# Gated mix of sliding-window attention and a GELU MLP: maxima begin sooner, V is kept by feature, and half of the repeated high parts are written by copies in DRAM

## The chip, the cores and the metric

The kernel runs on one core of one Trainium2 chip. The metric is the device time of one launch in microseconds; below it is 750.38 us, the median of three runs (749.24 to 751.35). The profile is of one further execution.

## What is computed

For x of 2048 rows and 512 features (all inputs in float32):

```python
g = sigmoid((x * gate_w).sum(-1, keepdims=True))
q, k, v = split_heads(x @ wqkv)              # 32 heads of 16 features
s = (q @ k.T) / 4, masked to 0 <= row - col < 256
a = merge(softmax(s) @ v) @ wo
b = gelu(x @ w1 + b1) @ w2 + b2              # 1792 hidden features
out = g * a + (1 - g) * b
```

## The kernel before, in words

The matrix products are made almost as exact as float32 from three products of rounded numbers: each operand is cut into a high part and a rest (both fp32r), and `mm3` (L107 to L110) issues high x high, high x rest, rest x high. Three such matmuls of 512 columns are called a step here (`MM3`); the dense work is a stream of steps.

**The order of the work is written out by one program.** `gated_mix` runs a model of time, `now`, in ns. `tick(ns)` lets it pass, `after(ns, fn)` puts an operation into a list by its due time, `need(key)` runs that list until something is done. Each engine executes its instructions in the order in which they were put out. `dense()` is a generator of all dense work: qkv for four quarters of 512 rows (`t` = 0 to 3), eight turns of the MLP (`TURNS`: half of the hidden features for one quarter; seven blocks of u, then four blocks of y), and the output projection (`final`, called a). `fill(ns)` takes that many ns of steps from it.

**Attention** runs over 8 groups of 4 heads (`g_`) and 16 blocks of 128 rows, 128 units `u` in all. After `fill(START)` a loop over the units begins. Each pass puts out four maxima (`att_max`, tile sm: a matmul of q and k, then DVE takes the row maximum with the mask added, L524), four scores (`att_exp`, tile st: a matmul that subtracts the maximum in its product, then ACT's exponential into tile pt, L586, and the cut of the window by POOL at L580, or by DVE at L574 for the last 12 units), and dense steps between them (2750 ns a pass before the first score, 2330 ns after). The maxima are `LEAD` = 12 units ahead of the scores. After every fourth unit `att_pvs` multiplies pt with V, 8 small tiles of 64 x 32 side by side in the array (L608, in plain float32, 96 records or, for the first rows of a group, 72). Column 16 of V is 1, so the same product gives the softmax's denominator. The sums (nd) go to DRAM, are divided there and back (`att_norm`) and come back as ot for the projection. When the loop ends, the rest of `dense()` follows.

**What lies where.** qkv writes q and k to DRAM (SQ, SK) as three parts, because attention's products take 48 rows: rest, high, high for q; high, rest, high for k. `qk_out` stores the first two parts with one DMA (L329) and the repeated high part with a second one from the same SBUF tile (L330). `qkv_v` evicts V of one block of 128 rows with four ACT instructions into a tile vx of 17 columns a head, the last set to 1 by POOL (L338), and stores it with three DMAs (L357, L359). `att_load_v` (L505) loads, for a group and a quarter, 128 x 8 x 34 numbers into one half of `vbuf`; a weight load of L608 takes 32 neighbouring columns. `load_qd`, `load_kd`, `load_ks`, `load_qs` load q and k of a group. All DMAs are issued by SP, in one queue, in program order. While the last quarter's qkv and the first MLP turn run, the MLP's weights are loaded and cut (`split`, L178 on ACT, L182 on DVE or POOL). PSUM holds three sm, three st and two dense tiles (d).

Of the kernel before, what the change touches and what calls it, by code (L numbers as in the profile page):

```python
# [9 lines left out]
F32 = mybir.dt.float32  # L10
F32R = mybir.dt.float32r
BF16 = mybir.dt.bfloat16
AF = mybir.ActivationFunctionType
# [4 lines left out]
S, D, F, H, DH, W = 2048, 512, 1792, 32, 16, 256  # L18
T = 512
NT = S // T  # L20
NB = T // 128
# [3 lines left out]
NG = H // 4  # L25
# [7 lines left out]
def gated_mix(ctx: ExitStack, tc: tile.TileContext, x, wqkv, wo, w1, b1, w2, b2, gate_w, out):  # L33
    nc = tc.nc
# [11 lines left out]
    def f32(ap):  # L46
        return ap.bitcast(F32)

    tt = cp.tile([128, 2 * RB, 32], F32, name="tt")
    mask = cp.tile([128, 320], BF16, name="mask")  # L50
    qs = cp.tile([128, 2, S], F32R, name="qs")
# [3 lines left out]

    idle = cs.tile([128, 320], BF16, tag="jm", bufs=1, name="idle")
    nc.gpsimd.memset(idle, 0.0)
# [3 lines left out]
    SK = [dr.tile([H // NC, 16, 3, NC, T], F32, name=f"SK{t}") for t in range(NT)]  # L61
    SV = [dr.tile([128, NB, 2, H // 2 * 17], F32, name=f"SV{t}") for t in range(NT)]
    XT = [dr.tile([NC, 128, 2, T], F32, name=f"XT{t}") for t in range(NT)]
# [17 lines left out]

    cut = cs.tile([128, 2, 64], F32, name="cut")
    nc.gpsimd.memset(cut, 3e38)
    for r in (0, 64):
# [15 lines left out]
    nc.gpsimd.memset(f32(nms), 0.0)  # L100
# [138 lines left out]

    xts, xrs = {}, {}  # L240

# [72 lines left out]
    def qk_out(t, j, p):  # L314

        dst, i = (SQ[t], j) if j < NC else (SK[t], j - NC)
        e = sb.tile([128, 2, T], F32R, tag="h", bufs=7, name=f"qke{t}_{j}")

        h = 1 if j < NC else 0

        def hi():
            nc.scalar.activation(e[:, h], p, AF.Copy)  # L322

        def lo():
            nc.vector.tensor_sub(e[:, 1 - h], p, f32(e[:, h]))  # L325

        def store():
            to = dst[:, :, :, i].rearrange("h d s c -> (h d) s c")
            nc.sync.dma_start(to[:, 0:2], f32(e))  # L329
            nc.sync.dma_start(to[:, 2], f32(e[:, h]))  # L330
            done.add(("qk", t, j))
        after(100, hi), after(700, lo), after(700 + HOLDQ, store)

    def qkv_v(t, b):
        xt = xts[t]
        vx = f32(sb.tile([128, 2, T], F32R, tag="h", bufs=7, name=f"vx{t}_{b}"))
        vx = vx.rearrange("p s t -> p (s t)")[:, 0:H * 17].rearrange("p (h c) -> p h c", c=17)
        nc.gpsimd.memset(vx[:, :, 16:17], 1.0)  # L338

        p = ps.tile([128, D], F32, tag="d", bufs=2, name=f"v{t}_{b}")  # L340
        ts = slice(b * 128, (b + 1) * 128)
        for c in range(NC):
            w = wt["v", c]
            mm3(p, xt[:, c, 0, ts], xt[:, c, 1, ts], w[:, 0], w[:, 1], c == 0, c == NC - 1)
            yield MM3
        def ev():
            to = vx[:, :, 0:16].rearrange("p (s i g a) d -> p i s g a d", i=2, s=2, a=2)
            by = p.rearrange("p (i a g s d) -> p i s g a d", i=2, a=2, s=2, d=16)
            for i in range(2):
                for s in range(2):  # L350
                    nc.scalar.activation(to[:, i, s], by[:, i, s], AF.Copy)
            after(HOLDQ, store)

        def store():
            flat = vx.rearrange("p h c -> p (h c)")
            n = H // 2 * 17
            nc.sync.dma_start(SV[t][:, b, 1], flat[:, n:2 * n])  # L357
            for r in (0, 64):
                nc.sync.dma_start(SV[t][64 - r:128 - r, b, 0], flat[r:r + 64, 0:n])  # L359
            done.add(("v", t, b))  # L360
        after(100, ev)
# [139 lines left out]
    def att_load_v(g_, c):  # L501
        need(*[("v", c, b) for b in range(NB)])
        vt = vbuf[:, c % 2]
        dst = vt[:, 0:NB * 68].rearrange("p (j c) -> p j c", c=34)
        nc.sync.dma_start(dst, SV[c].rearrange("p j s c -> p (j s) c")[:, :, 34 * g_:34 * g_ + 34])  # L505
        vts[g_, c] = vt

    def att_max(g_, b, i):

        if b % RB == 0 and (g_, b // RB) not in Ms:  # L510
# [9 lines left out]
                         start=True, stop=True)  # L520
        junk = cs.tile([128, 320], BF16, tag="jm", bufs=1, name=f"jm{g_}_{b}_{i}")

# [69 lines left out]
    def att_pvs(u):  # L592
# [12 lines left out]
        def mm(b, i, hf, q, e, rhs, start, stop):  # L605
            r = 64 * (1 ^ hf ^ i % 2)
            v = 68 * (b % NB) + 17 * (i % 2 * 2 + i // 2)
            nc.tensor.matmul(pv[r // 64][32 * i:32 * i + 32, q - c * T:e - c * T],  # L608
                             vts[g_, b // NB][r:r + 64, v:v + 32], rhs(r),
                             start=start, stop=stop, skip_group_check=True, tile_position=(r, 32 * i))  # L610
# [400 lines left out]
```

## Time and profile before

| | |
|---|---|
| median of three runs | 750.38 us (749.24 to 751.35) |
| the profiled execution | 752.58 us |
| its span, first to last instruction | 750.6 us |
| PE / DVE / ACT / POOL busy | 98% / 69% / 57% / 50% |
| granted TensorE clock | full throughout |
| DMA: packets, bytes | 179258, 172.10 MB; 56672 packets under 512 bytes |
| share of the DMA queue of SP | 81% of 16 engines' span |
| first maximum on PE | 119.9 us |
| first / last PV section on PE | 182.5 us / 699.5 us |

A row of a profile names the engine, the line, the operation and out<-in by the program's tile names. PEld is the loading of weights into the array, which overlaps PE; SPq is SP's issuing of a DMA. Matmul ends are modelled, so where PE stands still is read from how long equal stretches of work take, and from the list of waits, more than from the busy share.

### The profile page before, as it was taken

Reading aid. Unit: us, or ns where it says so; the run is one execution under the profiler, and the core shown is the slowest. Engines: PE = TensorE matmul, PEld = TensorE weight load, DVE = VectorE, ACT = ScalarE, POOL = GpSimd, SP = SyncE. Lnnn points to the kernel's source line nnn. Section 1 sums busy time; section 2 is a strip of 40 time slices with the busy share of each in tenths; the row PEclk is TensorE's granted clock in tenths of the full one; section 3 lists DMA queues with packets and bytes.
Section 4 is the critical chain, followed back from the end, with each engine's and each line's share of the span. In section 5 each row is a group of like instructions: output and inputs, shape, how many; then the busy total and the mean of one; then the engine's idle time right before and its main releaser. Section 6 shows DMA issues by size and latency. Waiting matters only on the chain.

```text
span 750.6 us, 17969 instructions
## 1 busy us (share of the span) xinstructions
PE 733.8 (98%) x6129; PEld 605.3 (81%) x6129; DVE 519.6 (69%) x1567; ACT 430.9 (57%) x972; POOL 372.0 (50%) x846
## 2 busy tenths in 40 slices
PE   8999999998999999999999999999999999999998
PEld 6888888876788888888887877888888888878787
DVE  4532325789758867986898689868867886784552
ACT  4434522358547845864696478547845854785541
POOL 4200000339756765786577657757865875630000
PEclk9999999999999999999999999999999999999999
DMA  9889798998995687799576889996799898538783
GB/s 315 328 275 402 258 387 274 254 316 186 272 253 141 153 242 203 186 226 263 143 180 167 214 230 219 253 243 153 179 259 246 203 237 217 135 88 263 226 265 115
DMA packets 179258, 172.10 MB, mean 229 GB/s; under 512 B 56672, under 2 KB 122976, under 8 KB 179168
## 3 DMA queue, kind: packets, MB, share of 16 engines
q1 hardware_dynamic: 179168, 170.97, 81.0%
q8 instruction: 48, 0.79, 0.5%
q14 instruction: 42, 0.34, 0.2%
HBM read 108.53 MB, written 62.39 MB: 228 GB/s over the span
## 4 chain that ended last, share of the span: by engine, by line
PE 83%; DMA 6%; DVE 4%; ACT 2%; issue 2%; SPq 1%; POOL 0%; DVEq 0%; ACTq 0%; POOLq 0%
PE sm L519 9%; PE st L564 8%; PE y L108 7%; PE pv_sm L608 6%; PE y L110 6%; PE y L109 6%; PE u L108 5%; PE u L109 5%; PE u L110 5%; PE qk L110 4%; PE qk L108 4%; PE qk L109 4%; PE v L108 2%; PE a L108 2%; PE v L110 2%
## 5 line engine op out<-in xcount | busy, mean ns | idle before, releaser
L524 DVE CUSTOM_DVE_ANT_0 jm<-sm,mask 128x320 bf16<-128x320 f32 (+4 forms) x512 | 237.9, 465 | 83.4 <-PE sm L519 55.7
L580 POOL TENSOR_SCALAR_AFFINE_SELECT pt<-pt 64x256 f32<-64x256 f32 (+1 forms) x538 | 225.8, 440 | 118.6 <-ACT pt L586 108.2
L586 ACT ACTIVATE pt<-st 128x320 f32<-128x320 f32 (+4 forms) x512 | 207.1, 425 | 131.7 <-PE st L564 128.4
L519 PE MATMUL sm<-kd,qd 96*128 96x320 f32 (+4 forms) x512 | 156.3, 308 | 6.1 <-DVE M L524 3.8
L564 PE MATMUL st<-qs,ks 128*128 128x320 f32 (+4 forms) x512 | 155.7, 307 | 1.2 <-ACT pt L586 1.2
L546 POOL CAST qs<-tt 4x256 fp32r<-4x256 f32 x256 | 126.2, 493 | 42.4 <-DVE tt L539 31.4
L519 PEld LDWEIGHTS sm<-kd,qd 96*128 96x128 f32 x512 | 96.1, 188 | 34.3 <-DVE M L524 10.9
L564 PEld LDWEIGHTS st<-qs,ks 128*128 128x128 f32 x512 | 97.2, 190 | 21.5 <-ACT pt L586 2.3
L108 PE MATMUL y<-w,h 128*128 128x512 f32 x224 | 89.9, 401 | 0.0
L110 PE MATMUL y<-w,h 128*128 128x512 f32 x224 | 88.4, 395 | 0.3 <-DVE h L737 0.3
L109 PE MATMUL y<-w,h 128*128 128x512 f32 x224 | 88.2, 394 | 0.0
L108 PE MATMUL u<-mx,w 128*128 128x512 f32 x196 | 80.0, 408 | 0.0
L109 PE MATMUL u<-mx,w 128*128 128x512 f32 x196 | 77.3, 394 | 0.0
L110 PE MATMUL u<-mx,w 128*128 128x512 f32 x196 | 77.2, 394 | 0.0
L608 PE MATMUL pv_st<-pt,vbuf 64*32 64x320 f32 (+4 forms) x1408 | 73.2, 346 | 2.5 <-DVE pt L574 1.3
L608 PE MATMUL pv_sm<-pt,vbuf 64*32 64x320 f32 (+4 forms) x1408 | 74.1, 346 | 0.1
L608 PEld LDWEIGHTS pv_sm<-pt,vbuf 64*32 64x32 f32 x1408 | 51.1, 106 | 19.1 <-issue 2.3
L325 DVE TENSOR_TENSOR qke<-qk,qke 128x512 fp32r<-128x512 f32 x32 | 22.1, 690 | 47.4 <-ACT qke L322 39.3
L322 ACT ACTIVATE qke<-qk 128x512 fp32r<-128x512 f32 x32 | 19.1, 598 | 55.6 <-PE qk L110 32.3
L110 PEld LDWEIGHTS y<-w,h 128*128 128x128 f32 x224 | 42.1, 188 | 10.7 <-DVE h L737 1.2
L608 PEld LDWEIGHTS pv_st<-pt,vbuf 64*32 64x32 f32 x1408 | 46.0, 106 | 2.8 <-DVE pt L574 1.5
L338 POOL MEMSET vx<- 128x32 f32 x16 | 2.4, 156 | 89.2 <-DMA SQ<-qke 42.9
(148 smaller groups left out, 1334.4 us busy)
## 6 DMA issues: line engine op xcount, KB each, us to landing
kd<-SK SPq DMA_DIRECT2D x32, 384.0 KB
qs<-SQ SPq DMA_DIRECT2D x64, 192.0 KB
mx<-XT SPq DMA_DIRECT2D x24, 512.0 KB
SQ<-qke SPq DMA_DIRECT2D x16, 512.0 KB
SK<-qke SPq DMA_DIRECT2D x16, 512.0 KB
ND<-nd SPq DMA_DIRECT2D x32, 256.0 KB
raw_w<-in_B_w_dram SPq DMA_DIRECT2D x28, 256.0 KB
ks<-SK SPq DMA_DIRECT2D x32, 192.0 KB
```

The lines of the kernel that those rows point to most:

```text
L108: nc.tensor.matmul(p, lh, rh, start=first, stop=False)
L109: nc.tensor.matmul(p, lh, rl, start=False, stop=False)
L110: nc.tensor.matmul(p, ll, rh, start=False, stop=last)
L322: nc.scalar.activation(e[:, h], p, AF.Copy)
L325: nc.vector.tensor_sub(e[:, 1 - h], p, f32(e[:, h]))
L519: nc.tensor.matmul(p[:, :w], qd[0:96, n, pr, 128 * j:128 * (j + 1)], kd[0:96, n, pr, k1 - w:k1], start=True, stop=True)
L524: nc.vector.tensor_tensor_reduce(junk[:, :w], p[:, :w], mask[:, 320 - w:320], 1.0, -3e38, ALU.add, ALU.max, M[:, 2 * (b % RB) + hb, pr:pr ...
L546: nc.gpsimd.tensor_copy(dst, src.unsqueeze(1).broadcast_to([4, 2, RB, 32]))
L564: nc.tensor.matmul(p[:, :w], ks[:, slot(g_, kb // NB), pr, at:at + 128], qs[:, pr, k0:k0 + w], start=True, stop=True)
L580: nc.gpsimd.affine_select(out=v, in_=v, pattern=[[0, v.shape[1]], [1 - 2 * e, 64]], compare_op=ALU.is_ge, fill=0.0, base=-e, channel_multi ...
L586: nc.scalar.activation(pt[:, hf, pr, :w], p[:, :w], AF.Exp, scale=SCALE)
L608: nc.tensor.matmul(pv[r // 64][32 * i:32 * i + 32, q - c * T:e - c * T], vts[g_, b // NB][r:r + 64, v:v + 32], rhs(r), start=start, stop=s ...
```

## The change

Three things change together.

1. `START` goes from 105000 to 97000 ns: the attention loop begins 8 us of dense work sooner. Nothing else in the loop changes.
2. V lies in DRAM by feature: per quarter, `SV` is [2, 128, 8, 128]; for a head parity, a row and a group it holds 16 features x 4 blocks x 2 heads. The four blocks of a quarter are evicted into two tiles that stay until the last block is done, with a step of 8 numbers between features, and are stored with three DMAs a quarter of 4 KB rows. A load for a group and a quarter has 256 pieces of 512 bytes. The ones are set once at the start, behind each of the four V regions of `vbuf`. A weight load takes every eighth number, 32 of them: 16 features, a one, and whatever lies behind (results of those 15 columns are not used). So that this stays finite, `cut` (now filled with 1e30) and `mask` lie in the same tile as V.
3. For the groups 4 to 7 (`i >= 2`), the repeated high part is not stored from SBUF. A DMA copies it from the first part in DRAM, with due times 188000, 196000, ... 308000 ns.

```diff
-    SV = [dr.tile([128, NB, 2, H // 2 * 17], F32, name=f"SV{t}") for t in range(NT)]
+    SV = [dr.tile([2, 128, NG, NB * 32], F32, name=f"SV{t}") for t in range(NT)]
...
+    vbuf = cs.tile([128, 4 * VB + 288], F32, name="vbuf")
+    cut = vbuf[:, 2 * VB:2 * VB + 128].rearrange("p (e x) -> p e x", e=2)
+    mask = vbuf[:, 4 * VB + 128:].bitcast(BF16)
...
-    vbuf = cs.tile([128, 2, NB * 68 + 16], F32, name="vbuf")
-    nc.gpsimd.memset(vbuf[:, :, NB * 68:], 0.0)
+    nc.gpsimd.memset(vbuf[:, 0:2 * VB], 1.0)
+    nc.gpsimd.memset(vbuf[:, 2 * VB + 128:4 * VB + 128], 1.0)
...
             nc.sync.dma_start(to[:, 0:2], f32(e))
-            nc.sync.dma_start(to[:, 2], f32(e[:, h]))
-            done.add(("qk", t, j))
+            if i < 2:
+                nc.sync.dma_start(to[:, 2], f32(e[:, h]))
+                done.add(("qk", t, j))
+            else:
+                copies[0] += 1
+                after(COPY0 + COPY * copies[0] - now[0], copy, to)
+
+        def copy(to):
+            nc.sync.dma_start(to[:, 2], to[:, h])
+            done.add(("qk", t, j))
...
-        nc.gpsimd.memset(vx[:, :, 16:17], 1.0)
...
-            for i in range(2):
-                for s in range(2):
-                    nc.scalar.activation(to[:, i, s], by[:, i, s], AF.Copy)
-            after(HOLDQ, store)
+            for s in range(2):
+                to = vxs[t, s].rearrange("p (i g d b a) -> p i g b a d", i=2, b=NB, a=2, d=16)
+                for i in range(2):
+                    nc.scalar.activation(to[:, i, :, b], by[:, i, s], AF.Copy)
+            if b == NB - 1:
+                after(HOLDQ, store)
...
+        k = (2 * VB + 128) * (c % 2)
+        vt = vbuf[:, k:k + 2 * VB].rearrange("p (s x) -> p s x", s=2)[:, :, 0:NB * 32]
+        nc.sync.dma_start(vt, SV[c][:, :, g_].rearrange("s p x -> p s x"))
...
-            v = 68 * (b % NB) + 17 * (i % 2 * 2 + i // 2)
+            v = vts[g_, b // NB] + VB * (i % 2) + 2 * (b % NB) + i // 2
...
-                             vts[g_, b // NB][r:r + 64, v:v + 32], rhs(r),
+                             vbuf[r:r + 64, v:v + 32 * 8 - 7:8], rhs(r),
...
+COPY0 = 180000.0
+COPY = 8000.0
+VB = NB * 32 + 8
...
-START = 105000.0
+START = 97000.0
```

What the smaller START moves on PE, at the first score (st_0_0, unit 0). Before, it stands in the third block of u of the first MLP turn, after the maxima of units 0 to 11:

```order
L110 MATMUL u_2_1740<-xt_1009,w_2_1421 128x512
L519 MATMUL sm_12_1_1770<-kd,qd 128x320
L564 MATMUL st_0_0_1774<-qs,ks 128x320
L108 MATMUL u_2_1740<-xt_1009,w_2_1421 128x512
L109 MATMUL u_2_1740<-xt_1009,w_2_1421 128x512
L110 MATMUL u_2_1740<-xt_1009,w_2_1421 128x512
L519 MATMUL sm_12_0_1789<-kd,qd 128x320
L564 MATMUL st_0_1_1794<-qs,ks 128x320
```

Of the change, the same place is in the last qkv block, just ahead of the first block of u:

```order
L111 MATMUL qk_7_1597<-xt_970,qk_427 128x512
L532 MATMUL sm_12_1_1622<-kd,qd 128x320
L577 MATMUL st_0_0_1628<-qs,ks 128x320
L109 MATMUL qk_7_1597<-xt_970,qk_427 128x512
L110 MATMUL qk_7_1597<-xt_970,qk_427 128x512
L111 MATMUL qk_7_1597<-xt_970,qk_427 128x512
L532 MATMUL sm_12_0_1643<-kd,qd 128x320
L577 MATMUL st_0_1_1646<-qs,ks 128x320
L109 MATMUL u_0_1652<-xt_970,w_0_1290 128x512
```

The dense work has moved back by about two blocks and a half against the attention. In the first stretch of u there are now 33 maxima, 33 scores and two PV sections, where there were 31, 21 and one.

On SP, at the loads of q for the first two maxima chunks (qd of group 0, quarters 0 and 1). Before, they stand behind loads of ks and two blocks of V of the third quarter:

```order
L475 DMA ks<-SK_84 48x7x128
L477 DMA ks<-SK_84 48x2x64
L357 DMA SV_89<-vx_1_1111 128x272
L359 DMA SV_89<-vx_1_1111 64x272 x2
L480 DMA qd<-SQ_79 48x8x128
L475 DMA qd<-SQ_79 48x7x128
L477 DMA qd<-SQ_79 48x2x64
L480 DMA qd<-SQ_80 48x8x128
L475 DMA qd<-SQ_80 48x7x128
L477 DMA qd<-SQ_80 48x2x64
```

Of the change:

```order
L331 DMA SQ_81<-qke_3_1013 128x2x512
L493 DMA qd<-SQ_79 48x8x128
L488 DMA qd<-SQ_79 48x7x128
L490 DMA qd<-SQ_79 48x2x64
L493 DMA qd<-SQ_80 48x8x128
L488 DMA qd<-SQ_80 48x7x128
L490 DMA qd<-SQ_80 48x2x64
L331 DMA SK_85<-qke_7_1037 128x2x512
L493 DMA ks<-SK_83 48x8x128
L488 DMA ks<-SK_83 48x7x128
L490 DMA ks<-SK_83 48x2x64
```

They now stand right behind the store of the third quarter's last q block; ks and V's stores come later.

At the end of the attention on PE, the last scores (st_15) and the first of the last PV section. Before, the MLP's last y matmul stands ahead of the last score:

```order
L109 MATMUL y_13_10414<-w_13_6717,h_13_10098 128x512
L110 MATMUL y_13_10414<-w_13_6717,h_13_10098 128x512
L564 MATMUL st_15_3_10474<-qs,ks 128x64
L608 MATMUL pv_3_sm<-pt_10_10237,vbuf 32x64
L608 MATMUL pv_3_st<-pt_15_10452,vbuf 32x64
```

Of the change, one step of y stands between them, and eleven more follow the section:

```order
L111 MATMUL y_12_10352<-w_8_6305,h_8_9857 128x512
L577 MATMUL st_15_3_10369<-qs,ks 128x64
L109 MATMUL y_12_10352<-w_9_6404,h_9_9908 128x512
L110 MATMUL y_12_10352<-w_9_6404,h_9_9908 128x512
L111 MATMUL y_12_10352<-w_9_6404,h_9_9908 128x512
L621 MATMUL pv_3_sm<-pt_10_10108,vbuf 32x64
L621 MATMUL pv_3_st<-pt_15_10342,vbuf 32x64
```

More of the change, by code (lines that the diff above doesn't have):

```diff
@@ L49, in gated_mix @@
     tt = cp.tile([128, 2 * RB, 32], F32, name="tt")
-    mask = cp.tile([128, 320], BF16, name="mask")
+    idle = cp.tile([128, 320], BF16, tag="jm", bufs=1, name="idle")
     qs = cp.tile([128, 2, S], F32R, name="qs")
@@ L80, in gated_mix @@
                                 compare_op=ALU.is_ge, fill=NEG, base=0, channel_multiplier=1)
-    cut = cs.tile([128, 2, 64], F32, name="cut")
-    nc.gpsimd.memset(cut, 3e38)
+    nc.gpsimd.memset(cut, 1e30)
     for r in (0, 64):
@@ L238, in clear_q @@
         nc.scalar.activation(v, nil.broadcast_to([128, 2 * T]), AF.Copy)
-    xts, xrs = {}, {}
+    copies = [0]
+    xts, xrs, vxs = {}, {}, {}
     def load_xr(t, bs=range(NB)):
@@ L335, in qkv_v @@
         xt = xts[t]
-        vx = f32(sb.tile([128, 2, T], F32R, tag="h", bufs=7, name=f"vx{t}_{b}"))
-        vx = vx.rearrange("p s t -> p (s t)")[:, 0:H * 17].rearrange("p (h c) -> p h c", c=17)
-        nc.gpsimd.memset(vx[:, :, 16:17], 1.0)
+        if b == 0:
+            for s in range(2):
+                v = f32(sb.tile([128, 2, T], F32R, tag="h", bufs=7, name=f"vx{t}_{s}"))
+                vxs[t, s] = v.rearrange("p s t -> p (s t)")
         p = ps.tile([128, D], F32, tag="d", bufs=2, name=f"v{t}_{b}")
@@ L502, in att_load_v @@
         need(*[("v", c, b) for b in range(NB)])
[L503 to L506, printed above, removed]
+        k = (2 * VB + 128) * (c % 2)
+        vt = vbuf[:, k:k + 2 * VB].rearrange("p (s x) -> p s x", s=2)[:, :, 0:NB * 32]
+        nc.sync.dma_start(vt, SV[c][:, :, g_].rearrange("s p x -> p s x"))
+        vts[g_, c] = k
     def att_max(g_, b, i):
@@ L520, in att_max @@
                          start=True, stop=True)
-        junk = cs.tile([128, 320], BF16, tag="jm", bufs=1, name=f"jm{g_}_{b}_{i}")
+        junk = cp.tile([128, 320], BF16, tag="jm", bufs=1, name=f"jm{g_}_{b}_{i}")
         def red():
```

17 lines of the change are left out of this document (9 added, 8 removed).

## The prediction

> **What bounds the kernel now.** I read the page first.
>
> ```profile
> span 750.6 us, 17969 instructions
> PE 733.8 (98%) x6129; PEld 605.3 (81%) x6129; DVE 519.6 (69%) x1567; ACT 430.9 (57%) x972; POOL 372.0 (50%) x846
> L524 DVE CUSTOM_DVE_ANT_0 jm<-sm,mask 128x320 bf16<-128x320 f32 (+4 forms) x512 | 237.9, 465 | 83.4 <-PE sm L519 55.7
> ```
>
> PE is busy for 98% of the span, and the maxima are DVE's costliest group. The matmul ends are modelled, so 98% does not say how many microseconds can still be won. For that I cut the dense work into its stretches: a turn of the MLP is seven blocks of u (its first product, 12 matmuls a block), then four blocks of y (21 each), eight turns over. A stretch of u and one of y both hold 84 dense matmuls of 512 columns; only the attention between them differs. A step is three dense matmuls. In the windows view the columns are length, busy time with instruction count of PE, PEld, DVE, ACT and POOL, granted clock, DMA share, GB/s. In order: u and y of the first turn, the shortest later u, a later y, u with y of turn 4, u of turn 5, u and y of the last turn, the output projection.
>
> ```profile
> 151.90:186.40 34.50, 31.49 (x210) 24.39 (x209) 30.85 (x93) 25.23 (x52) 20.89 (x37) 1.00 0.96 241
> 186.40:222.60 36.20, 34.78 (x344) 28.50 (x343) 24.17 (x85) 17.73 (x41) 24.65 (x62) 1.00 0.97 269
> 290.40:323.80 33.40, 33.40 (x320) 28.14 (x319) 29.93 (x93) 25.65 (x58) 23.01 (x48) 1.00 0.76 185
> 256.40:290.40 34.00, 34.00 (x343) 28.41 (x341) 23.42 (x83) 17.29 (x39) 22.49 (x60) 1.00 0.86 238
> 358.50:393.20 34.70, 34.03 (x321) 28.25 (x320) 30.46 (x93) 27.47 (x62) 23.94 (x50) 1.00 0.68 161
> 393.20:428.20 35.00, 34.43 (x341) 28.17 (x341) 26.90 (x90) 18.79 (x43) 24.56 (x61) 1.00 0.75 187
> 428.20:465.50 37.30, 35.51 (x321) 28.01 (x320) 32.96 (x98) 28.63 (x65) 23.66 (x50) 1.00 0.91 221
> 636.00:668.40 32.40, 32.27 (x305) 26.06 (x304) 26.44 (x72) 25.96 (x60) 19.45 (x39) 1.00 0.42 112
> 668.40:703.40 35.00, 31.98 (x405) 25.50 (x403) 19.37 (x41) 20.29 (x48) 0.00 (x0) 1.00 0.70 218
> 703.40:747.10 43.70, 43.70 (x212) 36.62 (x204) 21.20 (x33) 16.83 (x28) 0.00 (x0) 1.00 0.61 206
> ```
>
> The first u stretch holds 210 PE instructions against 320, yet takes 34.5 us against 33.4. The missing ones are score matmuls (st) and PV matmuls; these are their rows, st in the first u and in the one at 290.4, then L608 in both.
>
> ```profile
> 151.90:186.40 34.50, 6.82 (x21) 3.98 (x21) 8.38 (x20) 1.00 0.96 241
> 290.40:323.80 33.40, 9.97 (x34) 6.28 (x33) 12.86 (x33) 1.00 0.76 185
> 151.90:186.40 34.50, 1.98 (x72) 1.49 (x72) 1.00 0.96 241
> 290.40:323.80 33.40, 4.37 (x168) 3.04 (x168) 1.00 0.76 185
> ```
>
> What they cost PE, from its timeline: one 320-column sm or st each 0.15 us (333.39 to 333.54), and a PV section of 96 records 2.32 us (333.79 until y starts at 336.11).
>
> ```profile
> 333.39 0.31 PE L519 MATMUL sm<-kd,qd 96*128 96x320 f32 x1
> 333.54 0.31 PE L564 MATMUL st<-qs,ks 128*128 128x320 f32 x1
> 333.79 0.25 PE L608 MATMUL pv_st<-pt,vbuf 64*32 64x64 f32 x2
> 333.87 0.22 PE L608 MATMUL pv_st<-pt,vbuf 64*32 64x64 f32 x2
> 333.93 0.33 PE L608 MATMUL pv_st<-pt,vbuf 64*32 64x192 f32 x2
> 334.52 0.44 PE L608 MATMUL pv_st<-pt,vbuf 64*32 64x320 f32 x2
> 334.79 0.44 PE L608 MATMUL pv_st<-pt,vbuf 64*32 64x320 f32 x2
> 336.11 0.50 PE L108 MATMUL y<-w,h 128*128 128x512 f32 x1
> ```
>
> So without stalls the first u stretch would be 33.4 - 14 x 0.15 - 2.32 = 29.0 us: **5.5 us stand still there**. The first y is 36.2 against 34.0 + 0.3 for one sm and one st more: 1.9 us. The last u would be 33.4 - 16 x 0.15 = 31.0 (1.4 lost), and the last y, without 32 sm and with a third section, 34.0 - 4.8 + 2.3 = 31.5 (3.5 lost). The projection at the end has no gap (43.70 busy of 43.70). The waits of PE name who is late:
>
> ```profile
> PE sm L519 <- DVE M L524: 3.8, 10, 0.8
> PE pv_st L608 <- DVE pt L574: 1.3, 1, 1.3
> ```
>
> DVE holds sm buffers until their maxima are taken. In the first u stretch it is busy 30.85 of 34.5 us with 93 instructions, which leaves 0.04 us between two of them: no room. It has the maxima, the gelu of seven blocks and weight splits (L182) together, while PE's own work there is short. That, not a transfer, is the first thing late.
>
> **The change, part by part.**
>
> *Maxima sooner.* START falls by 8 us of dense work: the order puts every maximum and score 12 steps earlier, so the first u stretch now holds 33 maxima, 33 scores and two PV sections, exactly what the stretches at 290.4 and 358.5 hold. PE's work there is then 33.4 us instead of 29.0, and DVE gets 4.4 us more time for two more maxima and one more nd sum. The splits stay: four on DVE before and after. L182 in the first u, at 358.5 and at 428.2 (DVE, then POOL):
>
> ```profile
> 151.90:186.40 34.50, 3.76 (x5) 2.58 (x2) 1.00 0.96 241
> 358.50:393.20 34.70, 3.17 (x4) 0.00 (x0) 1.00 0.68 161
> 428.20:465.50 37.30, 4.32 (x6) 0.00 (x0) 1.00 0.91 221
> ```
>
> The row at 358.5 has the same attention and four splits on DVE: 34.7 us, 1.3 of stall. The row at 428.2 has six, and a DMA share of 0.91: 37.3 us, 3.9. The first u has four on DVE and two on POOL at a share of 0.96, so it is no nearer to the one than to the other: I take the middle, 2.6 us, which is **-2.9 us** (ends -4.2 and -1.6; -5.5 if no stall is left). The y behind it inherits less lag; the y behind the split-laden u at 358.5 took 35.0, 1.0 over its 34.0, so 1.9 becomes 1.0: **-0.9** (0 to -1.9). The maxima taken sooner lie in qkv of the last quarter, whose first four blocks get 16 maxima instead of 7.
>
> ```profile
> 113.10:124.90 11.80, 11.80 (x57) 9.82 (x56) 5.57 (x24) 2.67 (x8) 0.32 (x2) 1.00 0.79 228
> ```
>
> Nine more at 0.465 us and a read of 0.08 bring DVE to 10.5 us and, with 42 gaps of 0.04, 12.2; PE then works 11.8 + 9 x 0.15 = 13.2. It fits: 0 (to +1).
>
> At the end the attention finishes 11 steps before the MLP does. One step of y (0.7 us) now stands between the last score and the last PV section, which waited 1.3 us for its cut: -0.7. The projection's first load (L703), due two blocks into the last y, falls behind most exponentials instead of among them: about -0.5, an estimate, since ACT waits in order for it. Against it, the last u loses 14 more maxima (PE 28.8 us by the same sum) while ACT keeps its 25.96 us busy and 60 instructions, some 28.4 with gaps: ACT is then the bound, +0.7. Net **-0.5** (-2 to +2). The 8 us moved behind the attention are PE-bound and were PE-bound before; the projection's tail only gets more slack.
>
> *First maxima's loads.* SP issued qd of the first group at 114.11 and PE used it at 119.88.
>
> ```profile
> 102.09 1.10 SPq L329 DMA_DIRECT2D SQ<-qke  x1
> ...
> 114.11 0.53 SPq L480 DMA_DIRECT2D qd<-SQ  x1
> 119.88 0.20 PE L519 MATMUL sm<-kd,qd 96*128 96x64 f32 x1
> ```
>
> PE now wants it 12 steps of 0.68 us (43.70 us by 64 steps of projection), 8.2 us, sooner: at 111.7. In the new order qd stands right behind the store of qke_3, the row at 102.09, and ks and the V stores stand behind it. Six loads at 0.53 us are issued by about 106, still 5.7 us ahead: 0 us (up to +4 if they land late, since a maximum that waits holds all of PE behind it).
>
> *V by feature.* Twelve V stores a quarter become three; each of the 32 loads becomes 256 pieces of 512 bytes instead of 1024 of 136. No PE wait names vbuf or SV, so 0; SP's queue and the DMA engines gain room before 190 us, where their share is 0.96. If it does move PE, it moves it towards the bigger gain below. Sixteen memsets on POOL go, off the chain. The evictions now write with a step of 32 bytes: four of 0.28 us a block against 2.7 us of matmuls (four steps) and two buffers, hidden even at twice that (bounds 0 to +0.5).
>
> ```profile
> L351 ACT ACTIVATE vx<-v x64: 272/281/297, 35.1 to 139.1; 128x128 f32<-128x128 f32 x64
> ```
>
> Two memsets of 128x272 replace a small one in POOL's setup, ahead of the first weight copy, which PE waits for:
>
> ```profile
> 5.45 0.31 POOL L100 MEMSET nm<- 128x256 f32 x1
> 5.88 0.61 POOL L194 CAST qk<-raw_qk 128x512 fp32r<-128x512 f32 x1
> 6.55 0.74 PE L310 MATMUL qk<-ks,qk 128*128 128x256 f32 x4 [0.98 <-POOL qk L194]
> ```
>
> Two at the pace of the nm memset (next start 0.25 us later) for one at 0.18: **+0.35** (0.1 to 0.5), nothing hides it.
>
> *Weights with a step.* L608 now loads 32 columns that lie 32 bytes apart; before, they were neighbours. No load with a step is in the trace. The rows nearest:
>
> ```profile
> L608 PEld LDWEIGHTS pv_sm<-pt,vbuf 64*32 64x32 f32 x1408 | 51.1, 106 | 19.1 <-issue 2.3 <-DVE M L524 0.9 <-DVE nm L536 0.8
> L110 PEld LDWEIGHTS y<-w,h 128*128 128x128 f32 x224 | 42.1, 188 | 10.7 <-DVE h L737 1.2
> ```
>
> 96 columns more cost 82 ns, so 32 columns are 27 ns of the 106. Wide passes follow each other after 270 ns (334.52 to 334.79) and hide any of this; narrow ones after 80 and 60 (333.79, 333.87, 333.93), so with the first load three are open per section. At twice the time a column that is 3 x 27 ns x 32 sections = 2.6 us, at four times 7.8. I take 0, since loads run beside the matmuls and bring a column in 0.85 ns, slower already than the 0.47 ns at which a 320-column matmul reads its columns (0.15 us); ends 0 and +7.8. [...]
>
> *Copies in DRAM.* Sixteen stores of 128x512 leave the four quarters of qkv; sixteen copies are issued on SP between about 190 and 320 us, among transfers with shares of 0.76 to 0.97. Each reads what was stored 100 us or more before, so SP does not wait for it; behind it stand scores' and V's loads. 0, at worst +1.0, the stall by which 35.0 exceeds 34.0.
>
> **Sum.** -2.9 - 0.9 - 0.5 + 0.35 = -3.95 us. The profiled execution took 752.58 us (span 750.6), 2.2 above the median of the three runs; 752.58 becomes 748.6, the median 750.38 becomes **746.4**.
>
> **Rivals.** (1) *The weight step costs.* Slower: at four times a column, 746.4 + 7.8 = 754.2. It decides from a load of about 171 ns: 65 ns more x 3 x 32 = 6.2 us, which eats the gain and 0.3% more. For it: each column is read from another place; against: loads overlap wide passes. At twice, 749.0. (2) *DVE stays the bound*, because gelu, maxima and splits meet anyway, as at 428.2, and the y and the end give nothing: -1.6 + 0.35, 749.1; for it the DMA share of 0.96, against it the row at 358.5. (3) *Relief is worth more*: the stalls of the first u and y and 2 us at the end all go, since transfers are fewer: -5.5 - 1.9 - 2 + 0.35 = 741.3. (4) *START buys nothing*: qd lands late, PE waits up to 4 us in front of the first maximum, and DVE's crowd only moves: 749.1 + 4 = 753.1.
>
> **Chances.** Forecast (743.5 to 748.5) 0.50, (1) four times 0.10 and twice 0.08, (2) 0.16, (3) 0.08, (4) 0.08. A measurement here tells about 0.3%, 2.25 us, from no change. Faster by more: 0.46 + 0.08 of (3) = 0.54. Slower by more: 0.10 + 0.06 of (4) + 0.04 of (2) with the copies or the end at their worst = 0.20. Within: 0.26. Range 741.3 to 754.2: from (3) to (1).
>
> **What would show it.** Right: first u stretch near 36 us with 33 st, y after it near 35, last section's wait near 0.6, PEld L608 near 106 ns, sections still 2.32 us, first PE matmul of qk at about 6.9. Wrong: L608 loads over 130 ns or sections over 2.4; a PE wait on qd before the first maximum; new PE stalls of 2 us or more between 190 and 320 beside L340's copies; the last u above 32 us with ACT named.

## The result and the profile after

The changed kernel takes **755.56 us** (median of 15 runs, 752.34 to 760.43) against 750.84 us (15 runs, 748.60 to 754.88): 1.0056 times as long, 95% interval 1.0038 to 1.0074. That is 4.2 us slower; 4.0 us faster was forecast. The profiled execution took 755.56 us, with a span of 753.9 and a granted clock of 1.000 over the whole of it.

The page first. These rows answer to the ones that the prediction opened with.

```profile
span 753.9 us, 17844 instructions
PE 735.1 (98%) x6129; PEld 614.3 (81%) x6129; DVE 518.1 (69%) x1567; ACT 436.2 (58%) x972; POOL 368.4 (49%) x831
L537 DVE CUSTOM_DVE_ANT_0 jm<-sm,vbuf 128x320 bf16<-128x320 f32 (+4 forms) x512 | 238.1, 465 | 73.9 <-PE sm L532 42.7
L621 PEld LDWEIGHTS pv_sm<-pt,vbuf 64*32 64x32 f32 x1408 | 59.3, 139 | 12.9 <-issue 2.6
```

DVE has the same work, and waits 9.5 us less for it (73.9 us idle in front of the maxima instead of 83.4). Two durations have moved. A load of PV weights takes 139 ns instead of 106. ACT's eviction of V, which now writes with a step of 8 numbers, takes 480 ns instead of 281 (medians, the prediction has the row of before); no PE wait names it.

```profile
L361 ACT ACTIVATE vx<-v x64: 410/480/515, 35.3 to 141.4; 128x128 f32<-128x128 f32 x64
```

Then the stretches, in the windows view with the prediction's columns (length, busy time of PE, PEld, DVE, ACT and POOL, granted clock, DMA share, GB/s). In order: the first u, the y behind it, the third u, the y of turn 6, then the last u, the last y and the projection.

```profile
154.60:191.30 36.70, 35.70 (x320) 29.30 (x319) 33.82 (x102) 30.37 (x66) 32.34 (x61) 1.00 0.85 216
191.30:225.60 34.30, 34.30 (x345) 29.00 (x343) 23.05 (x81) 16.62 (x40) 20.81 (x54) 1.00 0.92 262
293.30:329.10 35.80, 34.21 (x319) 28.60 (x319) 30.03 (x96) 27.01 (x58) 26.02 (x57) 1.00 0.92 236
538.80:576.10 37.30, 34.61 (x345) 29.09 (x344) 25.57 (x88) 17.01 (x41) 21.07 (x53) 1.00 0.91 233
644.50:675.80 31.30, 29.62 (x289) 24.78 (x288) 21.29 (x48) 26.09 (x59) 7.31 (x20) 1.00 0.40 109
675.80:704.70 28.90, 27.30 (x298) 21.71 (x297) 13.79 (x28) 15.87 (x38) 0.00 (x0) 1.00 0.80 260
704.70:750.30 45.60, 44.07 (x204) 36.31 (x203) 23.53 (x36) 15.83 (x26) 0.00 (x0) 1.00 0.51 172
```

The first u and y are near what was forecast: 36.7 us (36.0) and 34.3 (35.0). But the third u, with the same matmuls as before, has gone from 33.4 to 35.8 us, the y of turn 6 from 34.0 (534 to 568 before, with one sm and one st less, 0.3) to 37.3, and the projection from 43.7 to 45.6. PE's waits say for whom:

```profile
PE sm L532 <- DVE nd L645: 4.8, 5, 2.7
PE st L577 <- ACT pt L599: 3.3, 2, 1.7
PE sm L532 <- DVE M L537: 2.9, 7, 0.6
PE a L111 <- DVE ot L722: 1.5, 2, 1.3
```

Before, none of PE's waits from the first u on was over 1.3 us, that for the cut of the last section. Now there are five gaps of 1.27 to 2.69 us: two behind nd, two for ACT's exponentials, one for ot. The longest, from DVE's timeline near 568 us (in brackets the idle time before the instruction and what ended it):

```profile
564.04 0.08 DVE L537 DVE_READ_ACCUMULATOR2_ANT M<- 128x1 f32 x1
567.74 0.83 DVE L675 TENSOR_TENSOR num<-num,rb 128x512 f32<-128x512 f32 x1 [3.61 <-DMA rb<-RD]
569.86 0.35 DVE L663 RECIPROCAL den<-den 128x32 f32<-128x32 f32 x1 [1.29 <-DMA den<-ND]
570.13 0.63 DVE L824 SCALAR_TENSOR_TENSOR yo<-y,ya 128x512 f32<-128x512 f32 x1
570.68 0.67 DVE L645 TENSOR_TENSOR nd<-nd,pv_sm 128x512 f32<-128x512 f32 x1
571.27 0.48 DVE L537 CUSTOM_DVE_ANT_0 jm<-sm,vbuf 128x320 bf16<-128x320 f32 x1
```

And SP's, for the two loads that DVE waited for:

```profile
559.60 0.58 SPq L671 DMA_DIRECT2D rb<-RD  x1
561.19 0.60 SPq L659 DMA_DIRECT2D den<-ND  x1
```

DVE works in order. From 564.1 to 571.3 us it takes no maximum, because the product with rb, the reciprocal of den, yo and nd stand ahead of it; PE fills its sm buffers and then stands for 2.69 us. The loads took 8.1 and 8.7 us (559.60 to 567.74, 561.19 to 569.86); where DVE waited elsewhere in this profile, they landed 5.0 to 7.9 us after their issue. Before, they had 7 to 11 us: over twelve of the sixteen pairs (those of the last two groups apart), DVE came to rb 7.5 to 11.2 us after its issue and to den 7.1 to 9.7 us after it, and had to wait for den twice, 1.2 and 0.3 us. Now it comes sooner. Of the kernel before:

```profile
292.65 0.58 SPq L658 DMA_DIRECT2D rb<-RD  x1
302.31 0.91 DVE L662 TENSOR_TENSOR num<-num,rb 128x512 f32<-128x512 f32 x1
```

The rb that SP issued at 292.6 before was used at 302.3; SP's issue is now at 287.2, 5.4 us sooner, and DVE's product at 292.2, 10.1 sooner, after a wait of 2.6 us.

### The profile page after: what moved, and what is told of

It reads as the page before. It is cut to its first block, busy times and chain, and to the rows that moved or that the text cites. A ratio compares the mean times of both kernels' runs of the same rounds, so it can differ in the third digit from the quotient of the medians.

```text
span 753.9 us, 17844 instructions
## 1 busy us (share of the span) xinstructions
PE 735.1 (98%) x6129; PEld 614.3 (81%) x6129; DVE 518.1 (69%) x1567; ACT 436.2 (58%) x972; POOL 368.4 (49%) x831
## 4 chain that ended last, share of the span: by engine, by line
PE 81%; DMA 8%; DVE 5%; SPq 3%; issue 2%; ACT 1%; POOL 0%; DVEq 0%; ACTq 0%
PE sm L532 8%; PE st L577 8%; PE y L109 6%; PE pv_sm L621 6%; PE y L110 6%; PE y L111 6%; PE u L109 5%; PE u L110 5%; PE u L111 5%; PE qk L111 4%; PE qk L109 4%; PE qk L110 4%; DMA kd<-SK 3%; PE pv_st L621 2%; PE v L109 2%
## 5 line engine op out<-in xcount | busy, mean ns | idle before, releaser
L537 DVE CUSTOM_DVE_ANT_0 jm<-sm,vbuf 128x320 bf16<-128x320 f32 (+4 forms) x512 | 238.1, 465 | 73.9 <-PE sm L532 42.7
L621 PEld LDWEIGHTS pv_sm<-pt,vbuf 64*32 64x32 f32 x1408 | 59.3, 139 | 12.9 <-issue 2.6
L621 PEld LDWEIGHTS pv_st<-pt,vbuf 64*32 64x32 f32 x1408 | 55.5, 139 | 0.8
L111 PEld LDWEIGHTS y<-w,h 128*128 128x128 f32 x224 | 42.1, 188 | 9.9 <-DVE h L750 0.2
L109 PEld LDWEIGHTS y<-w,h 128*128 128x128 f32 x224 | 42.5, 190 | 3.6 <-issue 2.7
```

The source lines that it names most:

```text
L109: nc.tensor.matmul(p, lh, rh, start=first, stop=False)
L111: nc.tensor.matmul(p, ll, rh, start=False, stop=last)
L537: nc.vector.tensor_tensor_reduce(junk[:, :w], p[:, :w], mask[:, 320 - w:320], 1.0, -3e38, ALU.add, ALU.max, M[:, 2 * (b % RB) + hb, pr:pr ...
```

## The experiments

Four theories. **A**: the weights read with a step are the loss. **B**: START itself is, because it lays the attention differently beside the MLP; B1 by DVE's waits for rb and den, B2 by the end, where ACT's exponentials and the split of ot are late. **C**: the copies in DRAM delay den. **D**: every shift loses, since all due times suit START 105000. Each run is compared with runs of the kernel before on the same chip.

### One part at a time

START alone:

```
-START = 105000.0
+START = 97000.0
```

> The kernel before with START lowered by 8000 and nothing else. Theory A (the loss is the read with a step: PEld loads of the PV weights took 139 ns instead of 106, PV sections 2.37 instead of 2.32 us): START alone keeps its relief of 4.0 us in the first u and y and loses little at the end, so about 750.8 - 3 = 748. Theory B (the loss is START's own: DVE waits for den at 294 and 568 us, with PE stalls of 1.4 and 2.9 us, and the last u is bound by ACT): the relief of 4.0 us is eaten, 750 to 752, and the PE stalls sm <- DVE nd near 294 and 568 us are there again. Theory C (the copies in DRAM delay den): 748, without the stall near 294.

Measured: 755.29 us, ratio 1.0055 (1.0037 to 1.0073). The whole loss is there without the new V layout and without a copy. The waits are the same too:

```profile
PE sm L519 <- DVE nd L632: 3.3, 4, 2.1
PE st L564 <- ACT pt L586: 3.2, 2, 1.6
PE a L110 <- DVE ot L709: 1.4, 2, 1.1
```

B holds. But these stalls alone, with the relief of the first u and y taken off, do not add up to 4 us. Cut into microseconds, the stretch from the gap at 567.74 to 569.81 on shows what the page hides (the column behind POOL is the granted clock):

```profile
568.00:569.00 1.00, 0.00 (x0) 0.00 (x0) 0.73 (x2) 0.00 (x0) 0.89 (x3) 1.00 1.07 291
569.00:570.00 1.00, 0.19 (x1) 0.19 (x2) 1.00 (x3) 0.00 (x0) 0.00 (x0) 1.00 0.96 318
570.00:571.00 1.00, 1.00 (x6) 0.87 (x6) 0.71 (x5) 0.44 (x1) 0.00 (x0) 1.00 1.00 170
571.00:572.00 1.00, 1.00 (x6) 0.94 (x5) 0.86 (x3) 0.59 (x2) 0.00 (x0) 0.67 0.91 192
572.00:573.00 1.00, 1.00 (x4) 0.77 (x3) 0.59 (x4) 0.28 (x1) 0.65 (x2) 0.50 0.60 186
573.00:574.00 1.00, 1.00 (x5) 0.91 (x4) 0.50 (x2) 0.34 (x1) 0.91 (x3) 0.50 0.39 105
574.00:575.00 1.00, 1.00 (x5) 0.81 (x4) 0.00 (x0) 0.10 (x1) 0.00 (x0) 0.62 1.00 163
575.00:576.00 1.00, 1.00 (x7) 0.87 (x6) 0.50 (x2) 0.44 (x1) 0.00 (x0) 1.00 0.52 98
```

After a gap of 2.08 us, **the granted clock is halved for 3.41 us**: PE starts four or five matmuls in a microsecond instead of seven. By the clock that costs another 1.7 us (half of 3.41), and PE reads 1.00 busy all the while. The profiled execution of the changed kernel had no such drop, others had: eight of its 15 runs have a mean clock of 0.999 or more and a median of 752.93 us, seven have 0.993 to 0.998 and 756.61 us. Of 31 runs of the kernel before beside this one, 27 had 0.999 or more; of START alone, 3 of 12.

V by feature and its ones alone (START 105000, no copies):

> V by feature with ones kept on the chip, START as before, no copies in DRAM. Theory A: at least 32 sections x 0.048 us = 1.5 us slower than before, 752.3 or more, with loads of 139 ns. Theory B and C: less than 0.5 us from before (751), whatever the loads take, since sections are 2% of a part of the time only.

Measured: 751.55 us, ratio 1.0010 (0.9998 to 1.0023), clock 0.999 or more in all 12 runs. That lies between the two expectations, and it is no more than a part of the loss.

The copies alone, on the kernel before:

> The kernel before with the sixteen later copies in DRAM alone. Theory C (a copy in front of the den load makes DVE and then PE wait, 1.4 us near 294, and more of the kind): 752 to 753. Theory A and B: within 0.5 us of before, 750.8, since no maximum comes sooner and den has the same room as before.

Measured: 750.37 us, ratio 0.9998 (0.9986 to 1.0010). C falls. No cost of the copies is seen.

The changed kernel with neighbouring weights:

```
-vbuf[r:r + 64, v:v + 32 * 8 - 7:8]
+vbuf[r:r + 64, v:v + 32]
```

> The changed kernel with one change: the PV weights are read from 32 neighbouring columns instead of 32 that lie 32 bytes apart. This takes the wrong columns of V and no ones, so the attention's values are not the reference's; instructions, bytes and order are the same. Theory A: loads go back to 106 ns, PV sections to 2.32 us, and the time falls from 755.6 by 1.5 us at least, by 4.7 if the step is the whole loss (751 or less). Theory B and C: loads go back too, but the time stays at 754 to 755.6, because the loss lies in stalls elsewhere.

Measured: 753.77 us, ratio 1.0032 (1.0011 to 1.0053); loads of 107 ns again, sections of 2.325 us. 1.8 us less than the changed kernel by the medians, with intervals that overlap, and 2.4 us still lost with the stalls in place. A is the smaller part.

### Later division

`DIVS` says how long after the issue of den's load the five steps of the division are due: the reciprocal, its store, the loads of num and rb, their product, and its store. The second half is for the last two groups.

```
-DIVS = ((5000, 7500, 13500, 20000, 22000), (4500, 5700, 8500, 17000, 18500))
+DIVS = ((9000, 10500, 17000, 26000, 28000), (4500, 5700, 8500, 17000, 18500))
```

> The changed kernel with the reciprocal of den, its store, the loads of num and rb and the product due 4000 to 6000 ns later in every group but the last (9000, 10500, 17000, 26000, 28000 in place of 5000, 7500, 13500, 20000, 22000). Theory B1 (DVE stands in order before den and rb, whose loads take 7 to 8 us near 567; PE then stalls 2.7 us, and after such a gap the granted clock is 0.50 for 3.4 us in part of the executions): the gaps near 294 and 568 us go, 4.0 us and about one drop of 1.7 us in two executions, so 755.6 becomes 751 to 752, with the mean clock at 0.999. Theory B2 (what START loses lies at the end, ACT's exponentials in the last u): 754 to 755, the clock as low as before. Theory A (only the weights' step): 755.6.

Measured: 752.91 us, ratio 1.0025 (1.0013 to 1.0037). The same two stretches, u at 293 and y at 538, in the windows view:

```profile
293.40:328.20 34.80, 34.24 (x320) 28.80 (x319) 29.30 (x94) 26.91 (x58) 26.08 (x56) 1.00 0.91 230
537.50:571.80 34.30, 34.30 (x344) 29.13 (x343) 24.91 (x87) 16.99 (x41) 20.55 (x52) 1.00 0.97 239
```

35.8 became 34.8 and 37.3 became 34.3; the waits for nd behind rb and den fell from 4.8 us to 0.2. B1 is shown: by the ratios 2.3 us of the loss were DVE's waits in order (two intervals that just miss each other), though the 751 to 752 us and the clock of 0.999 that B1 gave were not reached. Three gaps over 1 us are left, all at the end: 1.67 us before a score and 1.58 before another, for ACT, and 1.14 in the projection. The mean clock is still 0.998. The other 1.9 us are left to B2 and A together.

### A longer step of the attention

START 97000 kept, and the 8000 ns given back over the 128 steps, first in the changed kernel:

```
-STEP = 2330.0
+STEP = 2392.5
```

> The changed kernel with START 97000 kept and the step of the attention lengthened from 2330 to 2392.5 ns, so that 128 steps take the 8000 ns back and the attention ends where it ended before the change. Theory B2 (the end costs): the PE waits on pt in the last u and y (1.7 and 1.6 us), on ot (1.3 us) and their clock drops go: 755.6 - 4 = 751.5. Theory B1 (den and rb): the burst near 568 us is only met in another place; DVE still waits for den somewhere, 754 to 755, unless the shift happens to part the attention's loads from the MLP's there.

Measured: 755.16 us, ratio 1.0053 (1.0035 to 1.0070). The attention ended at the same place of the dense work as before the change, with no step of y behind the last score, yet the last PV section waited 3.5 us for its cut, where it had waited 1.3. The waits for den were there again (5.3 us on DVE, three times), and the longest of them, 2.9 us, stands on DVE just ahead of that cut.

> The changed kernel with both: later division and the longer step. If B1 and B2 both hold, all PE gaps over 1.3 us go, the granted clock is 1.000 in nearly all executions, the relief of the first u (4.0 us) stays and the weights' step still costs 1.5: 750.8 - 4.0 + 1.5 + 0.3 = 748.6. If neither holds: 755.

Measured: 755.34 us, ratio 1.0053 (1.0037 to 1.0070): PE's waits behind nd fell from 3.0 to 1.7 us, but the last section waited 3.9 us, and the clock was halved for 6.8 us with it.

> START 97000, later division, longer step and the copies in DRAM, but V by token with its ones in DRAM as before, so the PV weights are neighbours. By theory A the weights' step is worth 1.5 us (PV sections 2.32 instead of 2.37): 747.1, faster than both. If the step only matters beside other stalls: as e7, 748.6.

Measured: 755.16 us, ratio 1.0050 (1.0033 to 1.0067). The neighbouring weights gained 0.2 us here, not 1.5: the last section waited 4.3 us for the cut, whatever stood before it. The cut was late for the reason of B1. DVE's order has the reciprocal of den ahead of it, and DVE waits for that load:

```profile
700.36 0.35 DVE L659 RECIPROCAL den<-den 128x32 f32<-128x32 f32 x1 [3.51 <-DMA den<-ND]
701.77 0.28 DVE L583 TENSOR_TENSOR pt<-pt,cut 128x128 f32<-128x128 f32 x1
```

In the kernel before, the cut (at 700.78) stood ahead of the reciprocal (702.14). In the run with both, DVE stood 3.4 us at the same place. The later division leaves the times of the last two groups, the second half of `DIVS`, as they were; so these three runs say nothing against B1 or B2 away from the end.

### Between the two, and a stall made by hand

> The kernel before with the copies in DRAM, the later division and START at 101000, half way. Theory B (START pays in the first u and y, and loses where den, rb and, at the end, ACT's exponentials make PE wait over 1.5 us, each such gap being followed in part of the executions by 3.4 us at half clock): half the relief, 2 us, is kept, den and rb are no longer waited for, and the end has no gap over 1.4 us: 751.2 - 2 = 749, clock 0.999 or more. Theory D (any shift of START loses more than it gains, because the order was fitted to 105000): 751.5 or more.

Measured: 752.97 us, ratio 1.0034 (1.0022 to 1.0047). In its profile one gap of 2.4 us stands in the last y with 3.4 us of half clock behind it. The time misses B's 749, and this run alone would suit D.

> The same with START at 97000 and the step of the attention 2361 ns, so that half of the 8000 ns is given back over the attention. Theory B: relief of 3 to 4 us in the first u and y, and at the end neither ACT's last u nor the last PV section's wait is over 1.5 us, since the end lies between the one and the other: 748. Theory D: 752 or more; the gap at the last PV section of 3.5 us that the step of 2392.5 showed would then be there in part, about 2 us.

Measured: 750.72 us, ratio 1.0005 (0.9996 to 1.0014), between the two expectations. B's relief is kept, no gap is over 1.21 us, but the projection is as long as in the changed kernel:

```profile
698.80:744.50 45.70, 44.49 (x204) 36.29 (x204) 23.35 (x36) 16.01 (x27) 0.00 (x0) 1.00 0.56 192
```

To see the clock by itself, the kernel before with a standstill of DVE at four places:

```
+        for _ in range(15 if (g_, rb) in ((2, 0), (3, 0), (5, 0), (6, 0)) else 1):
             nc.vector.transpose(tt.rearrange(...), f32(nms).rearrange(...))
```

> The kernel before with four stalls put in by hand: DVE does the transpose of nm fifteen times instead of once (14 x 0.45 = 6.3 us) at four places, in the y stretches near 256, 323, 465 and 534 us, where DVE has 7 us to spare. DVE's standstill of 6.4 us near 568 in the runs of START gave a PE gap of 2.1 us, so four gaps of about 2 us are expected. If a gap costs only itself: 751.2 + 4 x 2 = 759 in every execution, with the clock at 0.999 as before. If the granted clock falls after such a gap (0.50 for 3.4 us, 1.7 us each): mean clock 0.993 to 0.996, a spread of executions by multiples of 1.7 us, and a median of 761 to 766.

Measured: 777.14 us (776.12 to 781.01), ratio 1.0369 (1.0349 to 1.0390), mean clock 0.981 to 0.985 in every run. The gaps were longer than meant, 4.1, 4.0, 4.4 and 5.5 us, together 18.1; the other 8.6 us of the 26.7 fit the clock (3.4 us at half speed once, 6.8 three times: 11.9 us lost at most, part of it inside the gaps). The last of them, in windows of 2 us:

```profile
560.00:562.00 2.00, 0.21 (x16) 0.00 (x0) 1.86 (x5) 0.00 (x0) 0.00 (x0) 1.00 1.12 284
562.00:564.00 2.00, 0.00 (x0) 0.00 (x0) 1.86 (x5) 0.00 (x0) 0.00 (x0) 0.62 0.83 100
564.00:566.00 2.00, 0.25 (x1) 0.26 (x2) 1.82 (x6) 0.69 (x2) 1.15 (x2) 0.50 0.00 1
566.00:568.00 2.00, 2.00 (x7) 1.71 (x8) 2.00 (x7) 0.87 (x2) 1.84 (x4) 0.50 0.00 0
568.00:570.00 2.00, 2.00 (x9) 1.72 (x9) 0.88 (x4) 0.50 (x2) 1.83 (x6) 0.67 0.66 143
```

The clock falls while PE stands still (562 to 564) and comes back by itself, 3.5 us after work is resumed at 565.75: the gap is the cause of the drop, not its effect.

### The step of the weights

```
+k = (1, 2, 4, 8)[g_ % 4]
-vbuf[r:r + 64, v:v + 32 * 8 - 7:8]
+vbuf[r:r + 64, v:v + 31 * k + 1:k]
```

> The changed kernel with PV weights of groups 0 and 4 read from neighbouring columns, of 1 and 5 at a step of two numbers (8 bytes), of 2 and 6 at four (16 bytes), of 3 and 7 at eight (32 bytes, as changed). All but the last read other columns than V's, so the attention's values are not the reference's. [...] If any step costs: 139 at two already. If it grows with the step: 111, 120, 139.

A single run, 755.60 us. The loads of groups 0 to 3, one row for each, from the line's own view (minimum, median and maximum in ns, first and last start in us):

```profile
L622 PEld LDWEIGHTS pv_sm<-pt,vbuf x176: 102/107/109, 170.4 to 224.0; 64*32 64x32 f32 x176
...
L622 PEld LDWEIGHTS pv_sm<-pt,vbuf x176: 103/107/115, 239.0 to 290.5; 64*32 64x32 f32 x176
...
L622 PEld LDWEIGHTS pv_sm<-pt,vbuf x176: 131/134/167, 307.0 to 359.7; 64*32 64x32 f32 x176
...
L622 PEld LDWEIGHTS pv_sm<-pt,vbuf x176: 132/137/173, 374.7 to 428.7; 64*32 64x32 f32 x176
```

Nothing for 8 bytes, some 27 to 30 ns for 16, no more for 32. So not every step costs, and the cost does not grow from 16 to 32 bytes. It sets in above 8 bytes and at 16 at the latest; no step between them was run, and why it sets in there was not shown. Sections follow: 2.325 and 2.327 us at one and two numbers, 2.37 at four and eight.

### Taking the end's loss away

In the last y of the changed kernel DVE idles 4.07 us in front of yo (704.87), and the splits of ot, which the projection needs, stand behind it. So the half stretch (START 97000, step 2361, later division, copies, old V) with one line more:

```
-LAND0 = 13500.0
+LAND0 = 10000.0
```

> START 97000, step 2361, later division, copies, V as before, and the split of ot for the projection due 10000 instead of 13500 ns after its load, so that it stands ahead of the last nd on ACT and DVE. If the relief of the first u and y is real and only given back at the end: the projection falls from 45.7 to 44.2 us or less and the time from 750.7 to 749.2 or less, faster than before (750.5). If the relief is no gain: within 0.5 us of 750.7, the wait appearing elsewhere.

Measured: **748.79 us, ratio 0.9971 (0.9958 to 0.9983)**: faster than the kernel before. First u, y behind it, last u, last y and projection, windows view:

```profile
154.10:191.20 37.10, 34.96 (x320) 28.58 (x318) 34.11 (x102) 30.34 (x67) 33.46 (x62) 1.00 0.91 245
191.20:225.10 33.90, 33.90 (x350) 28.20 (x341) 22.77 (x80) 16.28 (x39) 20.14 (x53) 1.00 0.93 259
637.70:669.60 31.90, 31.09 (x297) 24.85 (x296) 25.11 (x59) 27.45 (x62) 12.88 (x27) 1.00 0.39 106
669.60:699.20 29.60, 28.08 (x303) 22.04 (x302) 15.52 (x33) 16.36 (x41) 0.00 (x0) 1.00 0.78 248
699.20:742.80 43.60, 43.60 (x205) 36.56 (x204) 21.21 (x33) 16.23 (x27) 0.00 (x0) 1.00 0.58 200
```

The projection is back at 43.6 us without a gap. So D, that every shift loses, falls: with the due times around it moved too, the kernel with START 97000 is faster. No run has these due times with START 105000, so how much of the gain is START's is read from the stretches: the stall of the first u is 37.1 - 33.4 = 3.7 us, where it was 5.5, and the y behind it has lost its 1.9.

> The changed kernel (V by feature, weights at a step of 32 bytes) with the same step, later division and earlier split. If the step costs where nothing else is late: 32 sections at 0.03 to 0.05 us, and setup 0.3 us, so 1.3 to 1.8 us above the run with V as before. If the step is hidden: equal to it within 0.5 us.

Measured: 749.70 us, ratio 0.9977 (0.9964 to 0.9989): faster than before as well. By the medians V by feature costs 0.9 us here, by the ratios 0.5, and the intervals overlap. That it costs something is shown by the sections; how much of their 1.4 us reaches the end is not settled between 0.5 and 1.8.

## Why the prediction was wrong

Term by term, in us, for the profiled executions:

| step of the prediction | forecast | measured | from |
|---|---|---|---|
| stall of the first u | -2.9 | -2.2 | 36.7 - 33.4 = 3.3, was 5.5 |
| y behind it | -0.9 | -1.9 | 34.3, which is 34.0 + 0.3 |
| maxima in qkv, loads of qd | 0 | 0 | no PE wait for qd |
| later stretches of the attention | not in the sum | +5.4 | 35.8 - 33.4 and 37.3 - 34.3 |
| end | -0.5 | +1.2 | below |
| weights with a step | 0 | +1.4 | 24 sections x 0.048 + 8 x 0.030 |
| setup on POOL | +0.35 | +0.3 | v of the first quarter starts at 32.22, was 31.96; not clear of chance, see below |
| evictions of V with a step | 0 | 0 | 0.48 us each, was 0.28; no PE wait for them |
| copies in DRAM | 0 | 0 | copies alone: ratio 0.9998 |
| granted clock | not in the sum | 0 here; +1.0 in the mean of the runs | 0.9980 against 0.9994 (the 31 runs beside START alone) |

The sum is +4.2, the span grew by 3.3. Twelve sections lie inside the table's stretches and are counted twice, 0.5 us; the rest is not resolved, since the rows come from single executions. The first matmul of qk, 6.55 before and 7.00 now, stood at 6.76 and 7.45 in two other profiles with the old setup, and the eight runs of the changed kernel at full clock lie between 752.34 and 755.56 us. With 1.0 for the clock (3.41 us at half speed is 0.0023 of the mean; 0.9 drops a run against 0.3, 1.7 us each) the span's 3.3 comes to 4.3, near the 4.2 us of the ratio. That is in part luck: the profiled execution of the kernel before was 1.7 us above the median of 750.84, and that of the changed kernel is the slowest of the eight. The median of the eight is 2.1 us above the kernel before; the rest of the loss comes with the runs whose clock dropped.

**The step that failed** is the one that was never written: for the stretches between the first y and the last u the sum has no term, because "the 8 us moved behind the attention are PE-bound and were PE-bound before". That may hold of the matmuls moved and says nothing of the others. START moves the attention's loads against the MLP's on one SP queue, and DVE against both. The margin by which den and rb came in time was that DVE reached them late, 7.1 to 11.2 us after their issue, with loads that land after 5.0 to 8.7; it stood in the trace of before. START used it up (the rb near 292 us: 9.7 us after issue before, 5.0 and a wait now; START alone shows the same waits), and 4000 to 6000 ns of room put back by hand took PE's waits behind them from 4.8 to 0.2 us.

**The end** was priced with the right engine and too small a size: ACT was named as the bound of the last u at +0.7; with a gap of 1.7 us, the stall there is 31.3 - (33.4 - 31 x 0.15) = 2.55 (before: 1.4). The last y has 28.9 - (34.0 - 45 x 0.15) = 1.65 (before: 3.5), nearly all of it a second gap for ACT of 1.6: the last section's wait went altogether (1.3 us, 0.7 forecast). But "falls behind most exponentials instead of among them: about -0.5" had the wrong sign: the split of ot fell behind the last y's sum on DVE, which waits for PE, and the projection, whose tail "only gets more slack" in the prediction, lost 45.6 - 43.7 = 1.9 us. Together 6.1, where it was 4.9. The run with the earlier split took these 1.9 us away.

**The weights' step** lay at the near side of rival (1): 139 ns, under the 171 ns at which it would have decided, over the 130 that the prediction set as the sign of being wrong. Why a load at a step of 16 or 32 bytes takes longer, no run shows. My argument that loads hide beside matmuls held for the wide passes only: a PV matmul of 64 columns takes 243 ns where it took 226, one of 320 columns 431 and 430.

Rival (4), START buys nothing, gave about the right time, 753.1, for a reason that was not seen (qd late): that is luck. Rival (2) had the first u as nearly as the forecast did (-1.6 against -2.9, measured -2.2), but not the y behind it, which gave back 1.9 us where the rival had nothing. Rival (3) fails in the first u, where 3.3 us of stall are left.

## What to carry to other kernels

When an engine that works in order is relieved, look at what it used to reach late: every load behind it had that lateness as its margin, and the row to read is the time from a load's issue to the instruction that uses it, not the wait, which is zero until the margin is gone. A shift of one stream of work against another needs a term for every stretch in which the two run side by side, not only for the one that it is meant for. And a gap of PE can have a price of its own that stands in the granted clock and not in any wait: in the profiles here, 11 of the 12 gaps of 2.08 us or more were followed by half the clock for 3.41 us or twice that, which costs 1.7 us or twice that at most. Whether it was paid depended on where the gap fell (2.66 us in one window of the clock's grid had a drop, 2.69 us across two had none), so it differed from run to run; of the gaps of 1.67 to 1.69 us one in five had a drop behind it, of the smaller ones only a pair of 0.83 and 0.71 us within 2.6 us.

## What was not expected of the hardware

- **The clock after a gap.** In the 16 profiles of this case, gaps of TensorE inside the program were followed by a halved clock in none of 31 of 1.1 to 1.64 us, in 1 of 5 of 1.67 to 1.69 us, in 4 of 5 of 2.08 to 2.69 us, and in all 7 of 3.48 us or more. A drop lasted 3.413 us, or 6.827 us with five of these seven. One drop came after two gaps of 0.83 and 0.71 us within 2.6 us; a like pair in two other profiles had none. The traces show more of it. Every stretch between two changes of the clock is a whole multiple of 3.413 us (in the run with stalls 266.24, 68.27, 139.95, 64.85 and 204.80 us: 78, 20, 41, 19 and 60 times; in the profiles of the kernel before and of the changed one 747.52 us at full clock, 219 times), so in these traces the clock changes on a grid of that period. Counted by this grid, all 11 windows at full clock with 1.88 us or more of idle PE were followed by half the clock, 2 of 6 with 1.62 to 1.69 us, and none with 1.60 or less; this takes in every drop inside the program. The gap of 2.69 us in the changed kernel's profile is cut by a border of the grid and had no drop, the one of 2.66 us at the same place in the run with neighbouring weights lies in one window and had one. Two windows of each, the changed kernel first (idle is the length less PE's busy time):

```profile
566.51:569.92 3.41, 2.20 (x11) 1.54 (x10) 0.89 (x2) 0.89 (x3) 2.18 (x5) 1.00 1.09 239
569.92:573.34 3.42, 1.94 (x11) 1.76 (x12) 2.99 (x10) 0.77 (x2) 0.21 (x1) 1.00 0.83 208
566.60:570.02 3.42, 0.76 (x5) 0.32 (x4) 2.19 (x6) 0.32 (x1) 1.82 (x4) 1.00 0.87 221
570.02:573.43 3.41, 3.41 (x11) 2.93 (x11) 2.08 (x10) 1.31 (x3) 0.10 (x1) 0.50 0.90 216
```

By these counts, 1.88 us of idle time in a window were enough each time (START alone has just this much, in the gap at 567.74). Runs without a profile dropped too where the profiled one did not: five of the eleven of the half stretch have a mean clock of 0.997 or 0.998, though no gap in its profile is over 1.21 us; what their gaps were is not known.
- **Weights with a step.** In the run with four steps, a load of 32 columns of four-byte numbers took 107 ns at a step of one or two numbers and 134 to 137 ns at four or eight; a section of 96 PV matmuls took 2.325 us at one and 2.37 at eight, 2% more.
- **Writing with a step.** An ACT eviction of 128 x 128 numbers took 0.48 us where it wrote with a step of 32 bytes and 0.28 us where it wrote neighbours (medians, the two layouts of V).
